# Block diagonal products as 64-wide pairs on two quarters of the array

## The chip, the cores and the metric

The kernel runs on one core of one Trainium2 chip. The metric is the device time of one launch in microseconds; the medians below are over separate runs, and the profile shows one further execution.

## The reference, cut to what matters

The program is a delta-rule attention followed by two feed-forward layers. Shapes: 4 batches, 8 heads, 768 tokens, head size 48; the layers see 3072 tokens of width 384.

```
k_n = k / (norm(k) + 1e-06)
for t in range(S):                                   # S = 768
    y[:, :, t] = einsum('bhd,bhde->bhe', q[:, :, t], state)
    v_old = einsum('bhde,bhd->bhe', state, k_n[:, :, t])
    state = state + beta_t * einsum('bhd,bhe->bhde', k_n[:, :, t], v_t - v_old)
x = y as (3072, 384)
out = sum over 4 experts of p[:, e] * (relu(x @ w1[e]) @ w2[e])      # inner width 1024
gate = 1 / (1 + exp(-(out @ w_gate)));  val = out @ w_val             # inner width 1536
return (gate * val) @ w_out
```

## The kernel before, in words

The attention is done in 12 steps of 64 tokens (`NC`, `C`). Four batches give a step two tiles (`i` = 0, 1) of 128 partitions; a tile holds two batches, one in partitions 0 to 63, the other in 64 to 127, and 8 heads lie along the free axis. Keys and queries lie transposed in `KQ` (and `YQ`, `KS`): the first batch of a tile in rows 64 to 111, the second in rows 0 to 47.

For each step, tile and head the kernel forms the Gram matrix of the 64 keys with keys and queries (`g_mm`, L318). To serve both batches in one product it first copies the keys into a block diagonal tile, `bdG` (`fill_bd`, L289 and L290), whose other blocks are zero. VectorE scales and masks the results into `LP`. From there they go through DRAM to `Lpp`, where VectorE inverts the unit triangular matrices of many heads at once, row by row (`inv_ops`, the instructions on `itmp` and `Xpp`). The first four steps invert 32-wide halves only (`INV[r][1]` is true for them); the rest inverts 64-wide. The inverse comes back through DRAM into `Xbd`, again block diagonal and 128 wide (`x_in`, `put`), and for the first four steps the off-diagonal 32x32 block comes into `Ld` (`off_in`).

The chain of one step (`chain`) is: products of keys and state (`ks_task`, L499 and L500, tile `pk`), then, for the first four steps only, two half products (`half_task`, L512: part 0 with `Xbd`, part 1 with `Ld`, tile `pu`), then the product with the inverse (`tb_task`, L521, tile `pu`), the read-out (`y_task`, tiles `py` and `yt`) and the new state (`s_task`, tile `ps`). Each is done once for a tile of 8 heads; this is called a task below. `ks_task` already works with quarters: for each head one product from rows 64 to 111 into outputs 0 to 63, and one from rows 0 to 47 into outputs 64 to 127.

The layers take most of the time: products of 128x128 weights with 512 columns (L689 into `ph`, L726 into `acc`), in float32r, with each operand split into a high and a low part. The attention's own products are float32 and show up as two records each.

The order of all instructions is fixed when the program is built. A model of time (`T`, `pe_at`, `vec_at`) goes through the layers; `plan` gives each task a due time, and `slot` and `fill` emit the due tasks between two groups of the layers' products. The model counts an attention task as 1.7 us whatever it holds, so its order doesn't depend on how the task's products are written. Before the layers begin, `startup` does steps 0 and 1's Gram matrices, those of steps 2 and 3, the inverses of steps 0 and 1 and the chain of step 0, with products on zeros (`warm`, L884) between. Every engine runs its own instructions in order. SP and GpSimd issue the DMAs.

Of the kernel before, what the change touches and what calls it, by code (L numbers as in the profile page):

```python
# [9 lines left out]
F32 = mybir.dt.float32  # L10
# [16 lines left out]
P = 128  # L27
# [57 lines left out]
def moe_delta_kernel(  # L85
# [14 lines left out]
    nc = tc.nc  # L100
# [43 lines left out]
    KQi = [KQ[:, :, i] for i in range(2)]  # L144
    KS = ap_.tile([112, 2, H, C], F32, name="KS")
    bdG = ap_.tile([112, 2, H, P], F32, name="bdG")
    YQ = ap_.tile([P, 2, 2, H, C], F32, name="YQ")
    KI = ap_.tile([P, 2, 2, H, D], F32, name="KI")
    rhsA = ap_.tile([112, 2, H, D], F32, name="rhsA")
    rhsB = ap_.tile([P, 2, H, D], F32, name="rhsB")  # L150
    V = ap_.tile([P, 2, H, D], F32, name="V")
    R = ap_.tile([P, 2, H, D], F32, name="R")
    Y = [ap_.tile([P, 2, DM], F32, name=f"Y{n}") for n in range(2)]
    YT = ap_.tile([112, KT + 1, 2, P], F32, name="YT")
    Xbd = ap_.tile([P, 2, H, P], F32, name="Xbd")
    Ld = ap_.tile([P, 2, H, P], F32, name="Ld")
    LP = [ap_.tile([P, 2, 2, H, C], F32, name=f"LP{n}") for n in range(2)]
    Lts, Pts = [t[:, 0] for t in LP], [t[:, 1] for t in LP]
    Lpp = ap_.tile([P, HC, 3 * HC], F32, name="Lpp")
# [114 lines left out]
    ld_t, od_t, xd_t, pd_t = {}, {}, {}, {}  # L274
# [7 lines left out]
    def load_kq(c):  # L282
        (q[1] or q[0]).dma_start(out=KQ, in_=kq[c])
# [1 line left out]
    def load_ks(c):  # L285
        (q[1] or q[0]).dma_start(out=KS, in_=kq[c, :, 0])

    def fill_bd(bd, t, i, eng):
        eng(out=bd[64:112, i, :, 0:C], in_=t[i][64:112, 0])  # L289
        eng(out=bd[0:48, i, :, C:P], in_=t[i][0:48, 0])  # L290

    def load_ys(c):
        if c:
            (q[1] or q[0]).dma_start(out=YQ[64:112, 0], in_=kq[c, 64:112, 1])
            (q[1] or q[0]).dma_start(out=YQ[0:C, 1], in_=kq[c, 0:C, 1])
        kv = kt[c].rearrange("p (i h d) -> p i h d", i=2, h=H)
        (q[1] or q[0]).dma_start(out=KI[0:C, 0], in_=kv[0:C])
        (q[1] or q[0]).dma_start(out=KI[C:P, 1], in_=kv[C:P])
        pd = pd_t.pop(c).rearrange("p (i h t) -> p i h t", i=2, h=H)
        q[0].dma_start(out=YQ[0:C, 0], in_=pd[0:C])  # L300
        q[0].dma_start(out=YQ[C:P, 1], in_=pd[C:P])
# [7 lines left out]
    def bank(shape, name):  # L309
        turn[0] += 1  # L310
        p, tag = free[turn[0] % len(free)]
        return p.tile(shape, F32, tag=tag, name=name)

    def g_mm(i, hg, bd, kq_t):
        pg = bank([P, 4, 2, C], "pg")
        for j in range(4):
            h = hg * 4 + j
            nc.tensor.matmul(out=pg[:, j], lhsT=bd[0:112, i, h], rhs=kq_t[i][0:112, :, h], start=True, stop=True)  # L318
        return pg

    def g_l(pg, c, i, hg):
        hs = slice(hg * 4, hg * 4 + 4)
        vec.tensor_tensor(
            out=Lts[c % 2][:, i, hs],
            in0=pg[:, :, 0],
            in1=w_all[:, 2 * c + i, hs].unsqueeze(2).to_broadcast([P, 4, C]),
            op=ALU.mult,
        )
# [9 lines left out]
    def g_raw(pg, c, i, hg):  # L338
        hs = slice(hg * 4, hg * 4 + 4)
        nc.scalar.copy(out=LP[c % 2][:, :, i, hs].rearrange("p a h t -> p h a t"), in_=pg)  # L340
# [125 lines left out]
    def put(t, p0, c0, n, src):  # L466
        q[0].dma_start(
            out=t[p0 : p0 + n, :, :, c0 : c0 + n].rearrange("p i h t -> p (i h) t"),
            in_=src.rearrange("i h j t -> j (i h) t"),
        )  # L470

    def x_in(c):
        r, c2 = INV_OF[c]
        for bp in range(2):
            if INV[r][1]:
                for a in range(2):
                    put(Xbd, bp * C + a * HC, bp * C + a * HC, HC, xd_t[r][c2, a, :, :, bp])
            else:
                put(Xbd, bp * C, bp * C, C, xd_t[r][c2, :, :, bp])

    def off_in(c):
        r, c2 = INV_OF[c]
        if INV[r][1]:
            for bp in range(2):
                put(Ld, bp * C, bp * C + HC, HC, od_t[r][c2, :, :, bp])

    def scale_v(c):
        for i in range(2):
# [13 lines left out]

    def half_task(c, i, part):
        U = Y[c % 2][:, i].rearrange("p (h d) -> p h d", h=H)
        m = P - HC if part == 0 else P
        pu = bank([P, H, D], "pu")
        for h in range(H):
            if part == 0:
                lhsT, rhs = Xbd[:, i, h, 0:m], R[:, i, h]
            else:  # L510
                lhsT, rhs = Ld[:, i, h], U[:, h]
            nc.tensor.matmul(out=pu[0:m, h], lhsT=lhsT, rhs=rhs, start=True, stop=True)  # L512
        if part == 0:
            nc.scalar.copy(out=U[0:m], in_=pu[0:m])
        else:
            vec.tensor_tensor(out=R[:, i], in0=R[:, i], in1=pu, op=ALU.subtract)

    def tb_task(c, i):
        pu = bank([P, H, D], "pu")
        for h in range(H):  # L520
            nc.tensor.matmul(out=pu[:, h], lhsT=Xbd[:, i, h], rhs=R[:, i, h], start=True, stop=True)  # L521
        wv = w_all[:, 2 * c + i].unsqueeze(2).to_broadcast([P, H, D])
        vec.tensor_tensor(out=rhsA[0:C, i], in0=pu[0:C], in1=wv[0:C], op=ALU.mult)
        vec.tensor_tensor(out=rhsB[C:P, i], in0=pu[C:P], in1=wv[C:P], op=ALU.mult)
# [249 lines left out]
    def plan(t, fn, kind=""):  # L774
        todo.append((t, len(todo), kind, fn))
# [87 lines left out]
    def plan_g(c, t):  # L863
        plan(t, lambda: load_kq(c))
        for i in range(2):
            plan(t + 12, lambda i=i: fill_bd(bdG, KQi, i, nc.scalar.copy))

        def g_task(i, hg):
            pg = g_mm(i, hg, bdG, KQi)
            g_l(pg, c, i, hg)  # L870
            g_p(pg, c, i, hg)

        for n, (i, hg) in enumerate([(0, 0), (0, 1), (1, 0), (1, 1)]):
            plan(t + 14 + 2 * n, lambda i=i, hg=hg: g_task(i, hg), "pe")
        plan(t + 23, lambda: (l_out(c), l_off(c), p_out(c)))

    def startup():
# [10 lines left out]
        KQ1 = [YQ[0:112, :, i] for i in range(2)]  # L888
# [10 lines left out]
        l_init(1)  # L899
        vec.memset(zero.bitcast(F32), 0.0)  # L900
        nc.scalar.activation(out=nt_[:, 0, 0], in_=zero[:, :H].bitcast(F32), func=AF.Sqrt)
        for i in range(2):
            nc.gpsimd.memset(bdG[0:64, i], 0.0)
            vec.memset(bdG[64:112, i, :, C:P], 0.0)
        for t in (Xbd, Ld, rhsA[C:112], rhsB[0:C], KI[C:112, 0], KI[0:C, 1], Y[0][P - HC :], Y[1][P - HC :]):
            nc.gpsimd.memset(t, 0.0)
        warm(WARM)

        def norm_one(c):
            vec.tensor_tensor(out=kn[c], in0=kn[c], in1=kn[c], op=ALU.mult)  # L910
            norm_sum(kn[c], c, 1)

        pg = {}
        norm_one(0)
        fill_bd(bdG, KQi, 0, vec.tensor_copy)
        norms(0, 1)
        fill_bd(bdG, KQi, 1, nc.scalar.copy)
        for i, hg in tasks:
            pg[0, i, hg] = g_mm(i, hg, bdG, KQi)
            g_l(pg[0, i, hg], 0, i, hg)  # L920
        l_out(0)
        l_read(0)
# [1 line left out]
        KQ3 = [t[:112, : 2 * H * C].rearrange("p (a h t) -> p a h t", a=2, h=H) for t in dec_mem[2:4]]  # L924
        for i in range(2):
            sp.dma_start(out=KQ3[i], in_=kq[3, :, :, i])
        for i in range(2):
            fill_bd(Xbd, KQ1, i, nc.scalar.copy)
        for bp in range(2):
            o = bp * C  # L930
            nc.scalar.copy(out=Ld[o : o + HC, :, :, o + HC : o + C], in_=Lts[0][o : o + HC, :, :, HC:C])
        norm_one(1)
        for i, hg in tasks[:2]:
            pg[1, i, hg] = g_mm(i, hg, Xbd, KQ1)
            g_p(pg[0, i, hg], 0, i, hg)
        norms(1, 2)
        for i, hg in tasks[2:]:
            g_p(pg[0, i, hg], 0, i, hg)
            pg[1, i, hg] = g_mm(i, hg, Xbd, KQ1)
        q[0] = pool_q  # L940
        p_out(0)
        load_v(0)
        for i, hg in tasks:
            g_l(pg[1, i, hg], 1, i, hg)
            g_p(pg[1, i, hg], 1, i, hg)
        nc.gpsimd.memset(Xbd[64:112, :, :, 0:C], 0.0)
        nc.gpsimd.memset(Xbd[0:48, :, :, C:P], 0.0)
        p_out(1)
        load_ys(0)
        scale_v(0)  # L950
# [13 lines left out]

        q[0] = pool_q
        raw = [(c, i, t) for c, t in ((2, KQi), (3, KQ3)) for i in range(2)]
        for n, (c, i, t) in enumerate(raw):
            for _, j, u in raw[: 2] if n == 0 else raw[n + 1 : n + 2] if n else []:
                fill_bd(bdG, u, j, nc.scalar.copy)
            for hg in range(2):  # L970
                g_raw(g_mm(i, hg, bdG, t), c, i, hg)
            if i:
                scale_p(c)
                p_out(c)
# [49 lines left out]
    with tc.manual_schedule():  # L1024
# [11 lines left out]
        for c in range(4, NC, 2):  # L1036
            t = dec_mem[c // 2] if c < NC - 2 else dec_mem[2]
            o = 0.7 * c - 2.0
# [23 lines left out]
        for n, (kind, b, e, s0, ns) in enumerate(PHASES):  # L1062
            nf = NF1 if kind == "m1" else NF2
            part = unit_us(kind, ns) / (2 if kind == "m1" else 3)
            h = {}
# [93 lines left out]
```

## Time and profile before

| | us |
|---|---|
| median of 3 runs | 1516.54 |
| lowest and highest | 1514.53, 1518.94 |
| the profiled execution | 1512.61 |
| its span in the profile | 1510.8 |
| mean granted clock of TensorE | 0.981 |

The span runs from the first to the last instruction that the profiler saw; the rest of the execution's time lies around it. Records of TensorE overlap: a product is recorded for longer than it holds the engine, so the spacing of starts tells what one costs. A granted clock of 1.00 is TensorE's level of 2.4 GHz, 0.50 that of 1.2 GHz.

### The profile page before, as it was taken

Reading aid. Unit: us, or ns where it says so; the run is one execution under the profiler, and the core shown is the slowest. Engines: PE = TensorE matmul, PEld = TensorE weight load, DVE = VectorE, ACT = ScalarE, POOL = GpSimd, SP = SyncE. Lnnn points to the kernel's source line nnn. Section 1 sums busy time; section 2 is a strip of 40 time slices with the busy share of each in tenths; the row PEclk is TensorE's granted clock in tenths of the full one; section 3 lists DMA queues with packets and bytes.
Section 4 is the critical chain, followed back from the end, with each engine's and each line's share of the span. In section 5 each row is a group of like instructions: output and inputs, shape, how many; then the busy total and the mean of one; then the engine's idle time right before and its main releaser. Section 6 shows DMA issues by size and latency. Waiting matters only on the chain.

```text
span 1510.8 us, 23046 instructions
## 1 busy us (share of the span) xinstructions
PE 1468.1 (97%) x8801; PEld 1222.8 (81%) x8801; DVE 1066.9 (71%) x1905; ACT 574.4 (38%) x921; POOL 264.9 (18%) x293
## 2 busy tenths in 40 slices
PE   5799899999999999999999999999999999999998
PEld 5688777888888888888888888888888888888887
DVE  8877998846888766778766778757778754444553
ACT  4045444533333334333343333343433343433343
POOL 4241457530011200012110002220001210001000
PEclk8689999999999999999999999999999999999999
DMA  8586688675443675444584435495433463333221
GB/s 231 163 260 208 222 267 266 215 202 151 150 139 109 181 189 146 140 141 128 162 208 133 133 116 165 132 225 144 133 102 106 132 163 94 123 101 108 88 94 63
DMA packets 97749, 235.50 MB, mean 156 GB/s; under 512 B 23544, under 2 KB 29816, under 8 KB 95608
## 3 DMA queue, kind: packets, MB, share of 16 engines
q1 hardware_dynamic: 87352, 195.04, 43.2%
q0 software_dynamic: 10144, 38.94, 9.9%
q8 instruction: 69, 1.13, 0.3%
q14 instruction: 40, 0.33, 0.1%
q10 hardware_dynamic: 144, 0.07, 0.0%
HBM read 202.10 MB, written 27.97 MB: 152 GB/s over the span
## 4 chain that ended last, share of the span: by engine, by line
PE 86%; DVE 8%; DMA 3%; issue 2%; ACT 1%; SPq 0%; DVEq 0%; ACTq 0%
PE ph L689 43%; PE acc L726 33%; PE pu L521 3%; PE pg L318 2%; DVE Xpp L112 1%; DVE itmp L112 1%; PE pk L499 1%; PE ps L571 1%; DMA raw<-in_wp 1%; DVE ws L112 1%; DMA ls<-LP 1%; PE yt L534 1%; DVE hlo L112 1%; PE pu L512 1%; PE yt L535 1%
## 5 line engine op out<-in xcount | busy, mean ns | idle before, releaser
L689 PE MATMUL ph<-xhi,ws 128*128 128x512 f32 (+1 forms) x2064 | 635.4, 390 | 1.5 <-ACT xhi L756 0.8
L726 PE MATMUL acc<-hhi,ws 128*128 128x512 f32 (+1 forms) x1632 | 497.2, 387 | 0.0
L689 PEld LDWEIGHTS ph<-xhi,ws 128*128 128x128 f32 x2064 | 378.4, 188 | 77.2 <-ACT xhi L589 1.3
L689 PE MATMUL ph<-xlo,ws 128*128 128x512 f32 (+1 forms) x1032 | 398.2, 386 | 0.7 <-DVE xlo L112 0.7
L726 PEld LDWEIGHTS acc<-hhi,ws 128*128 128x128 f32 x1632 | 302.0, 189 | 59.3 <-ACT hhi L696 0.3
L112 DVE TENSOR_TENSOR ws<-raw,ws 128x768 fp32r<-128x768 f32 x308 | 298.3, 970 | 60.8 <-ACT ws L190 58.1
L726 PE MATMUL acc<-hlo,ws 128*128 128x512 f32 (+1 forms) x816 | 314.5, 385 | 8.3 <-DVE hlo L112 8.2
L190 ACT CAST ws<-raw 128x768 fp32r<-128x768 f32 x308 | 253.8, 830 | 83.5 <-PE acc L726 63.8
L696 ACT ACTIVATE hhi<-ph 128x512 fp32r<-128x512 f32 (+1 forms) x200 | 116.2, 581 | 418.6 <-PE ph L689 410.9
L689 PEld LDWEIGHTS ph<-xlo,ws 128*128 128x128 f32 x1032 | 194.2, 188 | 41.8 <-DVE xlo L112 2.6
L112 DVE SCALAR_TENSOR_TENSOR hlo<-ph,hhi 128x512 fp32r<-128x512 f32 (+1 forms) x200 | 132.6, 666 | 130.6 <-ACT hhi L696 130.5
L726 PEld LDWEIGHTS acc<-hlo,ws 128*128 128x128 f32 x816 | 154.0, 189 | 40.6 <-DVE hlo L112 10.2
L112 DVE TENSOR_TENSOR itmp<-Xpp,Lpp 128x120 f32<-128x120 f32 (+27 forms) x403 | 174.3, 445 | 9.7 <-DMA Lpp<-ls 3.8
L112 DVE TENSOR_TENSOR Xpp<-Xpp,itmp 128x120 f32<-128x120 f32 (+27 forms) x403 | 176.2, 449 | 5.1
L112 DVE TENSOR_TENSOR gv<-ph,sg 128x512 f32<-128x512 f32 x72 | 49.7, 691 | 94.7 <-PE ph L689 94.6
L705 ACT CAST hhi<-gv 128x512 fp32r<-128x512 f32 x72 | 44.6, 620 | 171.7 <-DVE gv L112 171.7
L753 POOL TENSOR_TENSOR ACC<-ACC,ctmp 128x512 f32<-128x512 f32 x36 | 50.1, 1393 | 321.1 <-DVE ctmp L112 320.5
L112 DVE TENSOR_TENSOR hlo<-gv,hhi 128x512 fp32r<-128x512 f32 x72 | 51.3, 713 | 49.4 <-ACT hhi L705 49.4
L703 ACT ACTIVATE sg<-ph 128x512 f32<-128x512 f32 x72 | 43.0, 597 | 76.7 <-PE ph L689 76.7
L373 POOL DMA_DIRECT2D ld<-LP x16 | 10.7, 670 | 333.5 <-DVE LP L112 333.5
L318 PE MATMUL pg<-KQ,bdG 112*128 112x128 f32 x320 | 45.2, 291 | 15.1 <-ACT bdG L290 10.8
L318 PEld LDWEIGHTS pg<-KQ,bdG 112*128 112x128 f32 x320 | 43.6, 205 | 20.0 <-ACT bdG L290 12.4
(163 smaller groups left out, 1104.7 us busy)
## 6 DMA issues: line engine op xcount, KB each, us to landing
raw<-in_wp SPq DMA_DIRECT2D x200, 384.0 KB, 3.1
raw<-w_d SPq DMA_DIRECT2D x108, 384.0 KB, 3.5
KQ<-in_kq SPq DMA_DIRECT2D x9, 896.0 KB, 7.9
pd<-LP POOLq DMA_DIRECT2D x12, 512.0 KB, 8.1
YQ<-pd POOLq DMA_DIRECT2D x24, 256.0 KB, 7.0
Lpp<-ld POOLq DMA_DIRECT2D x8, 768.0 KB, 13.5
pe<-p_d SPq DMA_DIRECT2D x23, 256.0 KB, 4.4
dec_a<-in_wp SPq DMA_DIRECT2D x15, 384.0 KB, 4.3
```

The costliest lines, as they stand in the source:

```text
L112: return fn(*args, **kw)
L190: nc.scalar.copy(out=w[:, 0], in_=t)
L318: nc.tensor.matmul(out=pg[:, j], lhsT=bd[0:112, i, h], rhs=kq_t[i][0:112, :, h], start=True, stop=True)
L499: nc.tensor.matmul(out=pk[0:C, h], lhsT=KS[C:112, i, h], rhs=rhsA[C:112, i, h], start=True, stop=True)
L512: nc.tensor.matmul(out=pu[0:m, h], lhsT=lhsT, rhs=rhs, start=True, stop=True)
L521: nc.tensor.matmul(out=pu[:, h], lhsT=Xbd[:, i, h], rhs=R[:, i, h], start=True, stop=True)
L689: nc.tensor.matmul(out=res[q], lhsT=lt, rhs=rt, start=(k == 0 and j == 0), stop=(k == KT - 1 and j == 2))
L696: nc.scalar.activation(out=hh, in_=res[0], func=AF.Relu)
L703: nc.scalar.activation(out=sg, in_=res[0], func=AF.Sigmoid)
L705: nc.scalar.copy(out=hh, in_=gv)
L726: nc.tensor.matmul(out=acc_t[d][:, :w], lhsT=lt, rhs=rt, start=(u == 0 and j == 0), stop=(u == nf - 1 and j == 2),)
L753: (nc.vector if e == NE - 1 else nc.gpsimd).tensor_tensor(out=a, in0=a, in1=t, op=ALU.add)
```

## The change

The tile `Xbd` becomes `XT`, 64 columns wide a head in place of 128, and `Ld` shrinks likewise: both batches' blocks lie in the same columns, one in partitions 0 to 63, the other in 64 to 127. Each product with them is done by `pair_mm` as two products of 64x64, one on the rows and outputs 0 to 63, one on 64 to 127. `half_task` now copies all 128 rows of its first half product; the last 32, which it left out before, meet zeros in `Ld`.

The Gram matrices of steps 0 to 3, which `startup` does, read the keys in place (`g_mm` with `HALF`): rows 64 to 111 into outputs 0 to 63 and rows 0 to 47 into outputs 64 to 127, with no block diagonal copy. From step 4 on they stay as they were (`g_bd`). So the fills of `bdG` and `Xbd` in `startup` go, as do the clears of `Xbd` and of the last rows of `Y`; `bdG` is cleared as a whole on GpSimd.

```diff
-    Xbd = ap_.tile([P, 2, H, P], F32, name="Xbd")
-    Ld = ap_.tile([P, 2, H, P], F32, name="Ld")
+    XT = ap_.tile([P, 2, H, C], F32, name="XT")
+    Ld = ap_.tile([P, 2, H, C], F32, name="Ld")
...
+    HALF = ((slice(0, C), slice(C, 112)), (slice(C, P), slice(0, D)))
...
+    def g_mm(i, hg, kq_t):
+        pg = bank([P, 4, 2, C], "pg")
+        for j in range(4):
+            h = hg * 4 + j
+            for to, at in HALF:
+                nc.tensor.matmul(
+                    out=pg[to, j], lhsT=kq_t[i][at, 0, h], rhs=kq_t[i][at, :, h], start=True, stop=True
+                )
+        return pg
+
+    def pair_mm(out, lhsT, rhs):
+        for o in (0, C):
+            nc.tensor.matmul(out=out[o : o + C], lhsT=lhsT[o : o + C], rhs=rhs[o : o + C], start=True, stop=True)
...
-                    put(Xbd, bp * C + a * HC, bp * C + a * HC, HC, xd_t[r][c2, a, :, :, bp])
+                    put(XT, bp * C + a * HC, a * HC, HC, xd_t[r][c2, a, :, :, bp])
             else:
-                put(Xbd, bp * C, bp * C, C, xd_t[r][c2, :, :, bp])
+                put(XT, bp * C, 0, C, xd_t[r][c2, :, :, bp])
...
             if part == 0:
-                lhsT, rhs = Xbd[:, i, h, 0:m], R[:, i, h]
+                pair_mm(pu[:, h], XT[:, i, h], R[:, i, h])
             else:
-                lhsT, rhs = Ld[:, i, h], U[:, h]
-            nc.tensor.matmul(out=pu[0:m, h], lhsT=lhsT, rhs=rhs, start=True, stop=True)
+                pair_mm(pu[:, h], Ld[:, i, h], U[:, h])
...
         for h in range(H):
-            nc.tensor.matmul(out=pu[:, h], lhsT=Xbd[:, i, h], rhs=R[:, i, h], start=True, stop=True)
+            pair_mm(pu[:, h], XT[:, i, h], R[:, i, h])
...
-        for i in range(2):
-            nc.gpsimd.memset(bdG[0:64, i], 0.0)
-            vec.memset(bdG[64:112, i, :, C:P], 0.0)
-        for t in (Xbd, Ld, rhsA[C:112], rhsB[0:C], KI[C:112, 0], KI[0:C, 1], Y[0][P - HC :], Y[1][P - HC :]):
+        for t in (XT, Ld, bdG, rhsA[C:112], rhsB[0:C], KI[C:112, 0], KI[0:C, 1]):
             nc.gpsimd.memset(t, 0.0)
...
         norm_one(0)
-        fill_bd(bdG, KQi, 0, vec.tensor_copy)
         norms(0, 1)
-        fill_bd(bdG, KQi, 1, nc.scalar.copy)
         for i, hg in tasks:
-            pg[0, i, hg] = g_mm(i, hg, bdG, KQi)
+            pg[0, i, hg] = g_mm(i, hg, KQi)
             g_l(pg[0, i, hg], 0, i, hg)
...
-        for i in range(2):
-            fill_bd(Xbd, KQ1, i, nc.scalar.copy)
...
-        nc.gpsimd.memset(Xbd[64:112, :, :, 0:C], 0.0)
-        nc.gpsimd.memset(Xbd[0:48, :, :, C:P], 0.0)
...
-        for n, (c, i, t) in enumerate(raw):
-            for _, j, u in raw[: 2] if n == 0 else raw[n + 1 : n + 2] if n else []:
-                fill_bd(bdG, u, j, nc.scalar.copy)
+        for c, i, t in raw:
             for hg in range(2):
-                g_raw(g_mm(i, hg, bdG, t), c, i, hg)
+                g_raw(g_mm(i, hg, t), c, i, hg)
```

VectorE's instructions at the program's begin, both kernels against each other (`L112` is the line of a helper through which all of VectorE's instructions go; `kn` holds the keys whose norms are summed into `w_all`):

```order
 L112 MEMSET pre_lo 128x512
-L112 MEMSET bdG 48x8x64 x2
 L112 TENSOR_TENSOR kn<-kn 128x768
 L112 TENSOR_REDUCE w_all<-kn 128x16
-L112 COPY bdG<-KQ 48x8x64 x2
 L112 TENSOR_TENSOR norm_tmp<-norm_tmp 128x16
```

Two clears and two copies are gone from in front of the norms; nothing else on VectorE changes its place.

TensorE's instructions from the begin to the first product with `Ld`, before:

```order
L884 MATMUL acc_129<-pre_lo 128x512 x11
L318 MATMUL pg<-KQ,bdG 128x128 x16
L318 MATMUL pg<-YQ,Xbd 128x128 x16
L318 MATMUL pg<-KQ,bdG 128x128 x16
L318 MATMUL pg<-dec_a,bdG 128x128 x8
L318 MATMUL pg<-dec_b,bdG 128x128 x8
L979 MATMUL acc_129<-Xpp 128x512 x4
L884 MATMUL acc_129<-pre_lo 128x512 x14
L512 MATMUL pu<-R,Xbd 96x48 x16
L512 MATMUL pu<-Y_112,Ld 128x48 x8
```

and of the change (the lines are those of the changed kernel):

```order
L899 MATMUL acc_129<-pre_lo 128x512 x11
L329 MATMUL pg<-KQ 64x128 x32
L329 MATMUL pg<-YQ 64x128 x32
L329 MATMUL pg<-KQ 64x128 x32
L329 MATMUL pg<-dec_a 64x128 x16
L329 MATMUL pg<-dec_b 64x128 x16
L983 MATMUL acc_129<-Xpp 128x512 x4
L899 MATMUL acc_129<-pre_lo 128x512 x14
L336 MATMUL pu<-R,XT 64x48 x32
L336 MATMUL pu<-Y_112,Ld 64x48 x16
```

Each group keeps its place and has twice as many products, half as wide; all later tasks with `Xbd` or `Ld` are replaced in the same way, and the products of the layers between them are untouched.

## Rows read from the trace of the kernel before

**Rows 1.** The page: busy time by engine, and the granted clock in 40 slices.
```profile
PE 1468.1 (97%) x8801; PEld 1222.8 (81%) x8801; DVE 1066.9 (71%) x1905; ACT 574.4 (38%) x921; POOL 264.9 (18%) x293
...
PEclk8689999999999999999999999999999999999999
```

**Rows 2.** The page: the chain that ended last, shares of the span by engine.
```profile
PE 86%; DVE 8%; DMA 3%; issue 2%; ACT 1%; SPq 0%; DVEq 0%; ACTq 0%
```

**Rows 3.** Stages: length, busy us of PE, PEld, DVE, ACT, POOL; granted clock, DMA share, GB/s.
```profile
66.90:74.90 8.00, 7.93 (x34) 7.44 (x34) 4.84 (x18) 0.00 (x0) 0.14 (x1) 0.50 0.60 167
107.70:118.00 10.30, 10.30 (x66) 10.08 (x66) 5.56 (x11) 2.11 (x4) 2.35 (x3) 0.50 0.90 304
131.00:220.00 89.00, 81.63 (x444) 69.89 (x443) 82.38 (x167) 45.42 (x81) 38.06 (x38) 0.98 0.73 228
220.00:1510.00 1290.00, 1283.22 (x7510) 1060.05 (x7508) 883.73 (x1379) 482.15 (x757) 176.99 (x195) 1.00 0.50 145
```

**Rows 4.** Waits of TensorE from 220 us on, the longest: total us, times, longest.
```profile
PE acc L726 <- DVE hlo L112: 2.2, 1, 2.2
```

**Rows 5.** Timeline of TensorE, a task with the inverse: start, length, instruction, count.
```profile
1255.88 0.39 PE L689 MATMUL ph<-xlo,ws 128*128 128x512 f32 x1
1256.11 1.88 PE L521 MATMUL pu<-R,Xbd 128*128 128x48 f32 x16
1257.81 0.71 PE L689 MATMUL ph<-xhi,ws 128*128 128x512 f32 x2
1258.36 0.40 PE L689 MATMUL ph<-xlo,ws 128*128 128x512 f32 x1
```

**Rows 6.** Timeline of TensorE, begin and end of a task of keys and state.
```profile
1252.55 0.39 PE L726 MATMUL acc<-hlo,ws 128*128 128x512 f32 x1
1252.87 0.25 PE L499 MATMUL pk<-rhsA,KS 48*64 48x48 f32 x1
1252.87 0.25 PE L500 MATMUL pk<-rhsB,KS 48*64 48x48 f32 x1
...
1253.93 0.73 PE L689 MATMUL ph<-xhi,ws 128*128 128x512 f32 x2
1254.50 0.40 PE L689 MATMUL ph<-xlo,ws 128*128 128x512 f32 x1
```

**Rows 7.** Timeline of TensorE, a first half product and what follows.
```profile
329.94 1.48 PE L512 MATMUL pu<-R,Xbd 128*96 128x48 f32 x16
331.24 0.70 PE L726 MATMUL acc<-hhi,ws 128*128 128x512 f32 x2
```

**Rows 8.** Chain of waits, step 0's end: start, length, what.
```profile
66.37 0.56 DVE R L112
66.97 3.65 PE pu L521 x16
...
71.18 3.28 PE pu L521 x16
...
75.02 1.88 PE py L546 x32
```

**Rows 9.** Chain of waits, the opening.
```profile
7.18 0.72 DVE bdG L112
7.94 0.94 DVE bdG L112
8.92 5.39 PE pg L318 x32
...
24.44 13.73 DMA ls<-LP
```

**Rows 10.** Chain of waits, step 1.
```profile
106.22 0.47 DVE R L112
106.73 2.75 PE pu L521 x16
...
111.54 3.28 PE pu L521 x16
```

More of the change, by code (lines that the diff above doesn't have):

```diff
@@ L286, in load_ks @@
         (q[1] or q[0]).dma_start(out=KS, in_=kq[c, :, 0])
-    def fill_bd(bd, t, i, eng):
-        eng(out=bd[64:112, i, :, 0:C], in_=t[i][64:112, 0])
-        eng(out=bd[0:48, i, :, C:P], in_=t[i][0:48, 0])
     def load_ys(c):
@@ L312, in bank, with fill_bd, g_bd @@
         return p.tile(shape, F32, tag=tag, name=name)
-    def g_mm(i, hg, bd, kq_t):
+    HALF = ((slice(0, C), slice(C, 112)), (slice(C, P), slice(0, D)))
+    def fill_bd(t, i):
+        nc.scalar.copy(out=bdG[64:112, i, :, 0:C], in_=t[i][64:112, 0])
+        nc.scalar.copy(out=bdG[0:48, i, :, C:P], in_=t[i][0:48, 0])
+    def g_bd(i, hg, kq_t):
         pg = bank([P, 4, 2, C], "pg")
@@ L317, in g_mm @@
             h = hg * 4 + j
-            nc.tensor.matmul(out=pg[:, j], lhsT=bd[0:112, i, h], rhs=kq_t[i][0:112, :, h], start=True, stop=True)
+            nc.tensor.matmul(out=pg[:, j], lhsT=bdG[:, i, h], rhs=kq_t[i][0:112, :, h], start=True, stop=True)
         return pg
+    def g_mm(i, hg, kq_t):
[10 more added lines that the diff above has]
+            nc.tensor.matmul(out=out[o : o + C], lhsT=lhsT[o : o + C], rhs=rhs[o : o + C], start=True, stop=True)
     def g_l(pg, c, i, hg):
@@ L484, in off_in @@
             for bp in range(2):
-                put(Ld, bp * C, bp * C + HC, HC, od_t[r][c2, :, :, bp])
+                put(Ld, bp * C, HC, HC, od_t[r][c2, :, :, bp])
     def scale_v(c):
@@ L504, in half_task @@
         U = Y[c % 2][:, i].rearrange("p (h d) -> p h d", h=H)
-        m = P - HC if part == 0 else P
         pu = bank([P, H, D], "pu")
@@ L508, in half_task @@
             if part == 0:
-                lhsT, rhs = Xbd[:, i, h, 0:m], R[:, i, h]
+                pair_mm(pu[:, h], XT[:, i, h], R[:, i, h])
             else:
-                lhsT, rhs = Ld[:, i, h], U[:, h]
-            nc.tensor.matmul(out=pu[0:m, h], lhsT=lhsT, rhs=rhs, start=True, stop=True)
+                pair_mm(pu[:, h], Ld[:, i, h], U[:, h])
         if part == 0:
-            nc.scalar.copy(out=U[0:m], in_=pu[0:m])
+            nc.scalar.copy(out=U, in_=pu)
         else:
@@ L865, in plan_g @@
         for i in range(2):
-            plan(t + 12, lambda i=i: fill_bd(bdG, KQi, i, nc.scalar.copy))
+            plan(t + 12, lambda i=i: fill_bd(KQi, i))
         def g_task(i, hg):
-            pg = g_mm(i, hg, bdG, KQi)
+            pg = g_bd(i, hg, KQi)
             g_l(pg, c, i, hg)
@@ L926, in startup @@
             sp.dma_start(out=KQ3[i], in_=kq[3, :, :, i])
-        for i in range(2):
-            fill_bd(Xbd, KQ1, i, nc.scalar.copy)
         for bp in range(2):
             o = bp * C
-            nc.scalar.copy(out=Ld[o : o + HC, :, :, o + HC : o + C], in_=Lts[0][o : o + HC, :, :, HC:C])
+            nc.scalar.copy(out=Ld[o : o + HC, :, :, HC:C], in_=Lts[0][o : o + HC, :, :, HC:C])
         norm_one(1)
         for i, hg in tasks[:2]:
-            pg[1, i, hg] = g_mm(i, hg, Xbd, KQ1)
+            pg[1, i, hg] = g_mm(i, hg, KQ1)
             g_p(pg[0, i, hg], 0, i, hg)
@@ L938, in startup @@
             g_p(pg[0, i, hg], 0, i, hg)
-            pg[1, i, hg] = g_mm(i, hg, Xbd, KQ1)
+            pg[1, i, hg] = g_mm(i, hg, KQ1)
         q[0] = pool_q
```

## The prediction

> **What bounds the kernel now.** I read the page first. TensorE is busy for 97% of the span and no other engine for more than 71% [rows 1]. The chain that ended last agrees: 86% of it is TensorE and 8% VectorE [rows 2]. A busy share alone is weak evidence, because products overlap, so I cut the span by stage [rows 3]. From 220 us to 1510 us TensorE is busy for 1283.22 of 1290 us at the full granted clock, VectorE for 883.73, ScalarE for 482.15. The longest wait of TensorE in that stretch is a single one of 2.2 us [rows 4]. So in this stretch every microsecond that TensorE's instruction stream gets shorter comes off the end. Before it the picture is another: from 131 to 220 us VectorE is busy for 82.38 of 89 us, and in 66.9 to 74.9 us and 107.7 to 118 us TensorE works at a granted clock of 0.50 [rows 3], which is its level of 1.2 GHz. A saving there is worth what the chain of work makes of it.
>
> The order of instructions on every engine is written out beforehand and the change leaves it as it was but for what it replaces. So I can cost each replaced group where it stands.
>
> **1. Products with the inverse, steps 2 to 11 (20 tasks of 8 heads).** A task has 8 products, 16 records in the profile (two passes of float32). In the timeline around 1256 us [rows 5] I read starts, since records overlap. The last product before the task starts 0.23 us ahead of it, which is the usual spacing; the task holds the engine from 1256.11 to 1257.81, 1.70 us; and the two products after it take 0.55 us (1257.81 to 1258.36), where twice the usual spacing is 0.46. Together 2.48 us. That is 106 ns a record, although only 48 columns are streamed: a 128-wide weight load for each sets the pace.
>
> The new form is 32 records in 16 pairs, each a 64x64 block on its own quarter. The trace of before has the same form already, in the product of keys and state [rows 6]: rows 64 to 111 into outputs 0 to 63 beside rows 0 to 47 into outputs 64 to 127, stationary 48x64, 48 columns streamed, 32 records a task. Both records of a pair start at 1252.87. The task starts 0.32 us after the product ahead of it, lasts 1.06 us to 1253.93, and the two products behind it take 0.57 us: 1.95 us. The change's pairs have 64 rows where these have 48, and lie on the other diagonal; I take the row's value for them. Saved: 2.48 - 1.95 = 0.53 us a task, 20 x 0.53 = 10.6 us.
>
> **2. The off-diagonal block, steps 2 and 3 (4 tasks).** Same shape as above before and after: 4 x 0.53 = 2.1 us.
>
> **3. The first half products, steps 2 and 3 (4 tasks).** These load only 96 columns. They hold the engine from 329.94 to 331.24, 1.30 us [rows 7], with the edges of rows 5 (0.23 and 0.55): 2.08 us. Saved 0.13 each, 0.5 us.
>
> Items 1 to 3 lie where TensorE has no slack: **13.2 us**.
>
> At the edges row and rule have to be weighed. The pairs start late by 0.32 - 0.23 = 0.09 us and the first products behind them lose another 0.57 - 0.55 = 0.02 us [rows 5, 6]; this is inside the 1.95 us. The Trainium skill, "TensorEngine Tiling (Array Packing)", section Key Properties, says that changing the tiling mode drains TensorE. That rule speaks against this change, which adds such switches; what it would make of the sum is the fourth rival below. The trace agrees that a switch costs something, about 0.11 us a task.
>
> **4. Opening, before the inverse of step 0.** VectorE copies two blocks for the first Gram matrix, 7.18 to 8.88 us, and TensorE starts on it at 8.92 [rows 9]. Both copies go, and the first half of the keys has landed by 7.18, so the first Gram products start up to 1.74 us sooner. The Gram products as such I cost at nothing: 64 records of quarters with 128 columns streamed against 32 whole ones; a whole one takes 5.39/32 = 168 ns there [rows 9], part of it at the lower clock, and a pair that costs no more than a whole one leaves the time as it is. If pairs cost double, 5.4 us more work would stand against it, and nothing would be gained here. What the start is worth depends on the transfers: the chain shows a 13.73 us transfer of the next blocks, 24.44 to 38.17 us [rows 9]. I take **1.7 us**; ends: 0 (the transfers stay where they are) and 3.4 (the norms, queued on VectorE behind the copies, give as much again). The other fills on ScalarE, the two clears on GpSimd and the two clears of Y lie beside these transfers, and I cost their going at nothing. GpSimd's clear of the block diagonal tile moves behind those of XT and Ld; it is needed first for step 4, far behind.
>
> **5. Step 0's products with the inverse.** After VectorE's last subtraction (66.37) come two tasks at the lower clock, 3.65 and 3.28 us, and then the first read-out at 75.02 [rows 8]. That read-out has 64-wide pairs at the same clock: 32 records in 1.88 us. With 1.88 for each task, 1.77 + 1.40 = **3.2 us** are saved; ends: 0 (the read-out then waits for VectorE's scaling) and 4.8 (1.06 each, as in rows 6 at the higher clock). The tasks of half products before it wait on no path: VectorE works through the inverse of step 1 until 66.37.
>
> **6. Step 1.** Its half products run before VectorE is done with the norms; its next subtraction starts at 106.22 [rows 10]. I cost them at nothing; what covers them is that VectorE work, and without it they would give some 2 us more. The two tasks behind it take 2.75 and 3.28 us [rows 10]; with 1.88 each: 0.87 + 1.40 = **2.3 us**; ends 0 and 3.9 (1.06 each again).
>
> Where these stalls go: VectorE's norms at 102 to 106 us and the transfers ahead of them are late next, and they move with the start.
>
> **Sum.** 13.2 + 1.7 + 3.2 + 2.3 = 20.4 us. The profiled execution took 1512.61 us (span 1510.8), so it would take 1492.2; the median shown, 1516.54, stands 3.9 us above it, so 1496.1, say **1496 us**. Its own range: 13.2 + 0 gives 1503.3, 13.2 + 3.4 + 4.8 + 3.9 = 25.3 gives 1491.2. The runs shown spread by 2 us to each side, so 1489 to 1505.5.
>
> **Rivals.**
> - *The start gives nothing* (0.17). VectorE is busy for 93% of 131 to 220 us [rows 3]; if its work or the transfers are not freed sooner, items 4 to 6 are waited away there. Against it: VectorE has 5.56 of 10.3 us in 107.7 to 118, so it waits for TensorE just there. Left: 13.2 us, 1503.
> - *The pairs don't run side by side* (0.04), the case on the other side. Place: every changed task. Then a task lasts 2 x 1.06 = 2.12 us, with its edges 3.01 against 2.48 and 2.08: 24 x 0.53 + 4 x 0.93 = 16.4 us more, steps 0 and 1 at 3.76 a task 2.1 us more, and nothing at the opening: 18.5 us slower, 1535. It decides from a pair spacing of (2.48 - 0.32 - 0.57)/16 = 99 ns on; rows 6 have 66. Against it: those pairs do start together, and the read-out, with all rows in use and only the columns halved, runs in pairs too [rows 8].
> - *The clock* (0.06). With shorter work in the start, the level of 2.4 GHz may come back later. One stretch like 107.7 to 118 us costs about half its 10.3 us [rows 3]; two more of them leave 10.1 us of gain, 1506. Against it: TensorE worked at 1.2 GHz through most of the start anyway.
> - *Full drains at the edges* (0.06). By that mechanism a task would start only when the product ahead had ended, 0.39 us after its start [rows 6], 0.07 later than the pairs of rows 6 do, and the next product only after the last pair's 0.25 us, at most 0.18 more than a pair's spacing of 0.07: up to 0.25 us more a task, 28 x 0.25 = 7 us, 1503. This is the rule of the page named above, taken at its fullest; the pairs of rows 6 have both edges in them and pay 0.11, so I give it little.
> - *More than that* (0.05): the start gives its upper ends, with the 2 us of the covered half tasks: 27.3 us, 1489.
>
> The forecast itself gets 0.62. The range that holds 8 in 10 takes in the start that gives nothing, the clock and the full drains: 1488 to 1508. A change of 0.3%, about 4.5 us, is what a measurement of this kernel can tell from none. Faster by more: 0.91, from all cases but the serial pairs, less a rest for a rival that comes together with another; same 0.04; slower 0.05.
>
> **What will show it.** Right: between 260 and 1265 us each task of the inverse lasts 1.06 us, with 32 records in pairs that start together, and the stretch from 220 us on is 13 us shorter. Item 4 is right if the first Gram product starts near 7.2 us, item 5 if the first read-out follows VectorE's subtraction by about 5.5 us in place of 8.65, item 6 if the two tasks of step 1 take under 2 us each. Wrong: pairs that start one after the other, a start that ends no sooner, or new stretches of 0.50 in the granted clock.

## The result, and the profile after

The changed kernel takes 1497.3 us in the median of 4 runs (1497.07 to 1498.53); the kernel before took 1515.53 in 4 runs beside them (1514.44 to 1518.94). The ratio is 0.9886, with a 95% interval of 0.9869 to 0.9902: some 18 us less. The profiled execution took 1497.07 us with a span of 1495.3, against 1512.61 and 1510.8 before. So the two traces stand 15.5 us apart and the medians 18.2: the profiled execution of before was a quick one, 2.9 us under its median. What is worked out below from the two traces adds up to 15.5.

The page of the kernel after: busy time by engine, the granted clock in 40 slices, and the shares of the chain that ended last.

```profile
PE 1440.4 (96%) x9569; PEld 1183.7 (79%) x9569; DVE 1063.0 (71%) x1901; ACT 566.4 (38%) x907; POOL 259.3 (17%) x288
...
PEclk8789999999999999999999999999999999999999
...
PE 85%; DVE 8%; DMA 3%; issue 2%; ACT 1%; SPq 0%; DVEq 0%; ACTq 0%
```

Beside [rows 1, 2]: TensorE has 768 records more and is busy for 27.7 us less. It is still the bound, and the other engines did not move much. The granted clock fell below full in the same slices as before.

The stages of the kernel after. The first and the last two windows answer to [rows 3]; the second is the stretch at the lower clock in step 1. Columns as in [rows 3].

```profile
66.90:74.90 8.00, 8.00 (x102) 6.20 (x100) 7.45 (x21) 0.48 (x1) 1.08 (x2) 0.50 0.69 160
104.20:111.00 6.80, 3.78 (x41) 3.69 (x41) 6.17 (x14) 2.84 (x5) 0.56 (x1) 0.50 1.03 349
131.00:220.00 89.00, 81.81 (x429) 69.27 (x429) 82.78 (x163) 43.59 (x78) 39.88 (x42) 0.98 0.74 236
220.00:1495.00 1275.00, 1266.07 (x7941) 1035.11 (x7939) 878.61 (x1373) 481.60 (x756) 174.10 (x192) 1.00 0.51 146
```

From 220 us to the end TensorE is busy for 1266.07 of 1275 us; before, it was 1283.22 of 1290. Its work shrank by 17.2 us and the stretch by 15: idle time grew from 6.8 to 8.9 us. (The window begins in work that lies up to 3.8 us apart in the two kernels, so for the sum a better mark is taken below, the first half product of step 2.) The stretch at 0.50 in step 1 lasts 6.8 us, from 104.2 to 111.0, in place of 10.3 [rows 3].

Timeline of TensorE in the kernel after, a task with the inverse in step 10, the counterpart of [rows 5]: start, length, instruction, count.

```profile
1244.77 0.39 PE L704 MATMUL ph<-xlo,ws 128*128 128x512 f32 x1
1245.08 1.14 PE L336 MATMUL pu<-R,XT 64*64 64x48 f32 x32
1246.15 0.73 PE L741 MATMUL acc<-hhi,ws 128*128 128x512 f32 x2
1246.72 0.40 PE L741 MATMUL acc<-hlo,ws 128*128 128x512 f32 x1
```

The task has 32 records and holds the engine from 1245.08 to 1246.15, 1.07 us in place of 1.70. It starts 0.31 us after the product ahead, and the next two take 0.57 us. Together 1.95 us: to the hundredth what [rows 6] gave for pairs with 48 rows on the other diagonal. Neither the 64 rows nor the diagonal made a difference. Taken record by record, the two of a pair start 7 ns apart, and the next pair starts 58 ns behind: the sign that the prediction named.

The same view in step 2, where the tasks stand early (the bracket is the idle time ahead, and what ended it):

```profile
283.42 1.13 PE L336 MATMUL pu<-R,XT 64*64 64x48 f32 x32 [0.23 <-DVE R L112]
...
286.75 1.14 PE L336 MATMUL pu<-R,XT 64*64 64x48 f32 x32
...
289.77 0.40 PE L704 MATMUL ph<-xlo,ws 128*128 128x512 f32 x1
291.59 0.33 PE L549 MATMUL yt<-YQ,rhsA 112*64 112x64 f32 x4 [1.42 <-issue]
```

Here the tasks are as short, but TensorE waits 0.23 us for VectorE ahead of the first and 1.42 us ahead of the read-out of the first (`yt`), which reads what VectorE makes of that task (`rhsA` and `rhsB`, written up to 291.49 us; the read-out starts at 291.59, so this wait too is VectorE's, though the view names no releaser). VectorE in this place, first of the kernel after:

```profile
282.81 0.55 DVE L112 TENSOR_TENSOR R<-R,pu 128x384 f32<-128x384 f32 x1
...
290.37 0.54 DVE L112 TENSOR_TENSOR rhsA<-pu,w_all 64x384 f32<-64x384 f32 x1
290.93 0.56 DVE L112 TENSOR_TENSOR rhsB<-pu,w_all 64x384 f32<-64x384 f32 x1
```

and of the kernel before:

```profile
286.60 0.55 DVE L112 TENSOR_TENSOR R<-R,pu 128x384 f32<-128x384 f32 x1
...
294.17 0.54 DVE L112 TENSOR_TENSOR rhsA<-pu,w_all 64x384 f32<-64x384 f32 x1
294.73 0.56 DVE L112 TENSOR_TENSOR rhsB<-pu,w_all 64x384 f32<-64x384 f32 x1
```

All three stand 3.79 to 3.80 us sooner than before. The start had given just that by then (the first half product of step 2 begins at 269.72 us in place of 273.51). So between 270 and 292 us VectorE's queue sets the pace, and what TensorE saved there became waiting.

The start, in the chain of waits of the kernel after; its counterparts are [rows 8] to [rows 10].

```profile
7.14 1.96 PE pg L329 x32
9.13 1.99 PE pg L329 x32
...
13.05 4.57 DMA ls<-LP
...
17.77 6.47 DMA Lpp<-ls
24.26 13.46 DMA ls<-LP
...
65.97 0.56 DVE R L112
...
66.57 1.95 PE pu L336 x32
...
69.24 1.88 PE pu L336 x32
...
71.84 1.88 PE py L561 x32
...
90.17 10.41 DMA raw<-in_wp
...
106.62 0.56 DVE R L112
...
107.22 1.95 PE pu L336 x32
...
111.28 1.06 PE pu L336 x32
```

The reader sees a gain that comes and goes. The first Gram products start 1.8 us sooner and end after 4 us, and their first blocks are written at 11.58 us in place of 14.75. Of these 3.2 us only 1.8 are the copies; the rest is mostly the clock, which stood at 0.50 from 8.8 to 12.2 us in the trace of before (the first 32 records took 5.39 us, the next 32 at 1.00 took 4.08) and at 1.00 in this one. But the second transfer of blocks on the chain lands at 24.26 + 13.46 = 37.72 us, where it landed at 38.17 before [rows 9]: 3.2 us became 0.45. VectorE's subtraction for step 0 starts 0.40 us sooner [rows 8]. The two tasks behind it last 1.95 and 1.88 us, and the first read-out follows the subtraction by 5.87 us in place of 8.65: 2.8 us won. Then a load of weights, issued at 90.17, lands at 100.58 us, where before one issued at 92.32 landed at 100.09 (92.32 + 7.77). The product of step 1 therefore starts at 107.22, half a microsecond later than before [rows 10]. The load was issued 2.2 us sooner but was 10.41 us on its way in place of 7.77; why it took longer, no run shows. All that the start had won is gone by then.

### The profile page after: what moved, and what is told of

The parts are those of the page before. It is cut to its first block, busy times and chain, and to the rows that moved or that the text cites. A ratio compares the mean times of both kernels' runs of the same rounds, so it can differ in the third digit from the quotient of the medians.

```text
span 1495.3 us, 24548 instructions
## 1 busy us (share of the span) xinstructions
PE 1440.4 (96%) x9569; PEld 1183.7 (79%) x9569; DVE 1063.0 (71%) x1901; ACT 566.4 (38%) x907; POOL 259.3 (17%) x288
## 4 chain that ended last, share of the span: by engine, by line
PE 85%; DVE 8%; DMA 3%; issue 2%; ACT 1%; SPq 0%; DVEq 0%; ACTq 0%
PE ph L704 43%; PE acc L741 34%; PE pu L336 2%; DVE Xpp L112 2%; PE pg L321 1%; DVE itmp L112 1%; DMA ls<-LP 1%; PE pk L516 1%; DMA raw<-in_wp 1%; DVE ws L112 1%; PE ps L586 1%; PE yt L549 1%; DVE hlo L112 1%; DMA Lpp<-ls 1%; DVE dec_b L112 1%
## 5 line engine op out<-in xcount | busy, mean ns | idle before, releaser
L112 DVE TENSOR_TENSOR ws<-raw,ws 128x768 fp32r<-128x768 f32 x308 | 298.9, 972 | 58.0 <-ACT ws L190 55.2
L112 DVE SCALAR_TENSOR_TENSOR hlo<-ph,hhi 128x512 fp32r<-128x512 f32 (+1 forms) x200 | 132.5, 666 | 130.4 <-ACT hhi L711 130.1
L112 DVE TENSOR_TENSOR itmp<-Xpp,Lpp 128x120 f32<-128x120 f32 (+27 forms) x403 | 174.1, 444 | 13.5 <-DMA Lpp<-ls 7.6
L112 DVE TENSOR_TENSOR Xpp<-Xpp,itmp 128x120 f32<-128x120 f32 (+27 forms) x403 | 175.7, 448 | 5.1
L112 DVE TENSOR_TENSOR gv<-ph,sg 128x512 f32<-128x512 f32 x72 | 49.7, 690 | 89.0 <-PE ph L704 88.9
L112 DVE TENSOR_TENSOR hlo<-gv,hhi 128x512 fp32r<-128x512 f32 x72 | 51.4, 714 | 49.4 <-ACT hhi L720 49.4
L336 PEld LDWEIGHTS pu<-R,XT 64*64 64x64 f32 x1024 | 35.0, 143 | 28.4 <-DVE R L112 18.2
L112 DVE TENSOR_TENSOR ctmp<-acc,pe 128x512 f32<-128x512 f32 x54 | 37.1, 687 | 27.5 <-PE acc L741 27.5
## 6 DMA issues: line engine op xcount, KB each, us to landing
Lpp<-ld POOLq DMA_DIRECT2D x8, 768.0 KB, 13.2
```

The costliest lines, as they stand in the source:

```text
L112: return fn(*args, **kw)
L336: nc.tensor.matmul(out=out[o : o + C], lhsT=lhsT[o : o + C], rhs=rhs[o : o + C], start=True, stop=True)
```

## The experiments

In each group the runs of the kernel before stood beside the experiments on the same chip: a median of 1516.19 us for four of them (the Gram matrices alone, the pairs alone, the column halves, the late Gram matrices), 1514.59 for the other four.

**Which half of the change gives the time.** First the Gram matrices alone: the kernel before, with the Gram products of steps 0 to 3 on quarters of the keys in place, and the products with the inverse left 128 wide.

```diff
-            pg[0, i, hg] = g_mm(i, hg, bdG, KQi)
+            pg[0, i, hg] = g_mm(i, hg, KQi)
```

> The kernel before with only the opening's change: Gram matrices of steps 0 to 3 read the keys in place, without block diagonal copies; the products with the inverse stay 128 wide. Theory (the gain of the change lies in the products with the inverse; the opening's is waited away, because the transfer of step 1's blocks lands at 37.7 us after the change where it landed at 38.2 before): within 2 us of the kernel before, 1513 to 1517 us, and the first subtraction of step 0's chain behind the inverse still at 65.5 to 66.5 us. Rival (the opening carries a share of its own): 1508 to 1512 us.

Measured: 1516.22 us (12 runs), ratio 0.9999 (0.9989 to 1.0009). The opening alone is worth nothing, to a thousandth. The time came as expected; the subtraction did not, it starts at 68.53 us in this trace (the last section comes back to this).

Then the counterpart: the kernel after, with block diagonal copies for the Gram matrices of steps 0 to 3, as before.

```diff
-            pg[0, i, hg] = g_mm(i, hg, KQi)
+            pg[0, i, hg] = g_bd(i, hg, KQi)
...
-            pg[1, i, hg] = g_mm(i, hg, KQ1)
+            pg[1, i, hg] = g_bd(i, hg, KQ1, bd1)
```

> The changed kernel with the opening put back: block diagonal copies for the Gram matrices of steps 0 to 3, while the products with the inverse and its off-diagonal block run as pairs. Theory (all of the gain is the pairs): 1497 to 1499 us, each task with the inverse 1.06 us behind 260 us. Rival (the opening carries a share): 1501 to 1505 us.

Measured: 1499.8 us (5 runs), ratio 0.9883 (0.9867 to 0.99), that is, the whole gain of the change within the interval. The median lies 0.8 us above the range of the theory and 1.2 below that of the rival, so by itself this run leaves room for a small share of the opening; the first run, whose interval is 1.5 us to each side, leaves none that can be measured. Together: the time comes from the 64-wide pairs.

**What makes a pair run side by side.** In the first of two kernels each product with the inverse keeps the block diagonal tile and all 128 rows, and only its columns are cut in two. (It has the opening of the first experiment, and its first half products write all 128 outputs.)

```diff
+    def col_mm(out, lhsT, rhs):
+        for o in (0, C):
+            nc.tensor.matmul(out=out[o : o + C], lhsT=lhsT[:, o : o + C], rhs=rhs, start=True, stop=True)
```

> As the run with only the opening changed, but each product with the 128-wide inverse or off-diagonal block is cut in two by columns alone: all 128 rows into outputs 0 to 63, then all 128 rows into outputs 64 to 127. Theory (a task is paced by the weight loads, and halves of the columns load side by side): the task lasts 1.06 us as with quarters, 1496 to 1500 us. Rival (records run side by side only if their rows differ too): pairs one after the other, 1.7 us a task or more and the edges on top, 1515 us or more.

Measured: 1498.63 us (4 runs), ratio 0.9882 (0.9863 to 0.99), in the range of the theory. The timeline of TensorE of this kernel, one task:

```profile
1249.56 1.14 PE L335 MATMUL pu<-R,Xbd 128*64 128x48 f32 x32
1250.63 0.72 PE L744 MATMUL acc<-hhi,ws 128*128 128x512 f32 x2
```

The task holds the engine for 1.07 us, as the quarters do, and its records start in the same rhythm, 7 ns within a pair and 58 ns from pair to pair. So it isn't the smaller array quarter that counts: two column halves suffice, though both use every row. The Trainium skill, "TensorE: Matmul & The Clock Gate", section Part 3: Packing small matmuls (The mechanism), says that a weight load overlaps with products in flight only when their row groups differ. This trace doesn't bear that out: the row groups here are the same, and the pair still takes 67 ns (1.07 / 16), against the 106 ns of one 128-wide record [rows 5] and the 112 ns of two on the same quarter (next run).

In the second kernel everything is as after, but the order: the 8 heads of a task first all on the lower quarter, then all on the upper.

```diff
+    def halves_mm(pu, lhsT, rhs):
+        for o in (0, C):
+            for h in range(H):
+                nc.tensor.matmul(
+                    out=pu[o : o + C, h], lhsT=lhsT[o : o + C, h], rhs=rhs[o : o + C, h], start=True, stop=True
+                )
```

> The changed kernel with the products of a task in another order: all 8 heads on the quarter of rows 0 to 63 first, then all 8 on the quarter of rows 64 to 127, so that neighbours use the same quarter. Theory (the gain comes from two neighbours loading weights side by side): neighbours on one quarter go one after the other, 32 records at 58 to 66 ns, 1.86 to 2.1 us a task in place of 1.06, 28 tasks on the busy stretch: 22 to 29 us slower than the changed kernel, 1519 to 1526 us. Rival (half as many columns make the loads short enough by themselves): 1.06 us a task and 1497 to 1499 us.

Measured: 1522.38 us (4 runs), ratio 1.0045 (1.0027 to 1.0063). Its timeline, one task:

```profile
292.47 1.87 PE L523 MATMUL pu<-R,XT 64*64 64x48 f32 x32
294.27 0.72 PE L743 MATMUL acc<-hhi,ws 128*128 128x512 f32 x2
```

The same 32 records now take 1.80 us, 56 ns each, one after the other. A 64-wide record alone is thus quicker than a 128-wide one (106 ns), but two in a row are not (112): narrower loads by themselves give nothing. The time is above the kernel before's, and 25 us behind the kernel after. The products are the same, so the gain lies in what stands next to each: neighbours on the same quarter run one after the other, neighbours on different columns side by side (in the run ahead of this one with all rows shared). The expectation on the time held, and the task came out a little shorter than its lower end. This is the rival with serial pairs, made real: it does end on the other side. The forecast for that rival was 1535, because it doubled the 1.06 us of a task to 2.12, where 1.80 came.

A kernel with the rows halved and all 128 columns kept, two products added into the same outputs, wasn't tried, so nothing is shown on neighbours that differ in their rows alone.

**Why the later Gram matrices stay block diagonal.** The kernel after, with quarters for the Gram matrices of steps 4 to 11 too, and without the copies for them.

```diff
-        for i in range(2):
-            plan(t + 12, lambda i=i: fill_bd(KQi, i))
...
-            pg = g_bd(i, hg, KQi)
+            pg = g_mm(i, hg, KQi)
```

> The changed kernel with the Gram matrices of steps 4 to 11 in quarters too, and without their block diagonal copies on ScalarE. Theory (with 128 columns streamed a pair takes about 0.12 us, as in the opening of the changed kernel, where a whole block diagonal record takes 0.10 to 0.11): 8 pairs of a task of 4 heads last 0.95 to 0.98 us in place of 0.81, the edges add 0.1, 32 tasks: 6 to 9 us slower than the changed kernel, 1503 to 1507 us. Rival (paced by the weight loads like the products with the inverse): 0.53 us a task, 32 x 0.17 = 5 us faster, 1491 to 1493 us.

Measured: 1504.8 us (5 runs), ratio 0.9924 (0.9909 to 0.9938): 7.5 us slower than the kernel after, as the theory said. TensorE in one Gram task of this kernel:

```profile
421.65 0.39 PE L704 MATMUL ph<-xlo,ws 128*128 128x512 f32 x1
421.97 1.09 PE L329 MATMUL pg<-KQ 48*64 48x128 f32 x16
422.99 0.74 PE L741 MATMUL acc<-hhi,ws 128*128 128x512 f32 x2
```

and in the kernel after, with the block diagonal copy:

```profile
422.39 0.40 PE L741 MATMUL acc<-hlo,ws 128*128 128x512 f32 x1
422.62 1.05 PE L321 MATMUL pg<-KQ,bdG 112*128 112x128 f32 x8
423.43 0.72 PE L704 MATMUL ph<-xhi,ws 128*128 128x512 f32 x2
```

With 128 columns streamed a pair takes 1.02 / 8 = 128 ns, and a whole record 0.81 / 8 = 101 ns. There is nothing to win, and the edges come on top. A task costs some 0.3 us more (0.21 in itself, 0.09 ahead of it); over the 24 tasks behind 271 us that is 7 us. The copies on ScalarE that it saves win nothing back there. From the first half product of step 2 to the end of the span it is 1504.8 - 271.93 = 1232.9 us in place of 1225.6: 7.3 more. The two spans are 9.5 us apart; the other 2.2 us were there already at step 0's subtraction (68.19 us in place of 65.97; see the last section).

**Where the start's gain went.** Two suspects were in the trace of the kernel after: 1.8 MB of keys and queries for steps 2 and 3, queued ahead of small transfers of blocks at about 13 to 24 us; and SyncE's queue at 84 to 90 us. The first kernel moves the loads behind the stores of step 1's blocks.

```diff
-        load_kq(2)
...
-            sp.dma_start(out=KQ3[i], in_=kq[3, :, :, i])
...
         l_off(1)
+        load_kq(2)
...
+            sp.dma_start(out=KQ3[i], in_=kq[3, :, :, i])
         l_read(1)
```

> The changed kernel with three loads moved in SP's queue: the keys and queries of steps 2 and 3 (1.8 MB) are issued behind the stores of step 1's blocks, not ahead of them. Theory (the opening's gain was lost because those stores, issued from 21 us on, stood behind the loads and landed at 37.7 us): the stores land before 32 us, the inverse of step 1 starts 3 to 4 us sooner, and the first subtraction behind it comes at 62 to 63.5 us in place of 66.0; of that 2 to 4 us reach the end, 1493 to 1496 us. Rival (the weight loads at 90 to 106 us set the pace of the start again, whatever comes before): the subtraction comes sooner, the time stays at 1496.5 to 1499 us.

Measured: 1495.41 us (4 runs), ratio 0.9869 (0.9852 to 0.9885), not to be told from the kernel after. Its chain (of an execution of 1500.49 us, the longest of the four):

```profile
31.95 9.60 DMA Lpp<-ls
...
65.11 0.56 DVE R L112
...
89.28 11.12 DMA raw<-in_wp
```

The blocks had landed by 31.1 us in place of 37.7, but the next transfer on the chain then took 9.60 us in place of 4.15. It landed at 41.55 us, where it had landed at 42.48, and so the subtraction came at 65.11 us in place of 65.97, and not at 62 to 63.5. The median lies in the range of the theory, but its mechanism fell in part: the next transfer took over the wait (that it competes with the moved loads is likely, but no run shows it). And the weight load again ended what was left: the product of step 1 starts at 107.04 us.

The second suspect. SyncE's queue in the kernel after:

```profile
84.01 0.39 SPq L182 DMA_DIRECT2D raw<-in_wp  x1
89.09 0.38 SPq L632 DMA_DIRECT2D dec_a<-in_kt  x1
89.52 0.60 SPq L683 DMA_DIRECT2D pe<-p_d  x1
90.17 0.42 SPq L182 DMA_DIRECT2D raw<-in_wp  x1
```

The queue stands from 84.4 to 89.1 us at a load of norm keys, which waits until its tile has been used for the keys loaded before; the weight loads wait behind it. This kernel gives that load a tile of its own.

```diff
+    kn_last = ap_.tile([P, 4 * DM], F32, name="kn_last")
...
-            t = dec_mem[c // 2] if c < NC - 2 else dec_mem[2]
+            t = dec_mem[c // 2] if c < NC - 2 else kn_last
...
-                back["dec"].append((o + 0.6, "", lambda t=t: norm_load(t, NC - 2)))
+                back["dec"].append((o + 0.6, "", lambda: norm_load(kn_last, NC - 2)))
```

> The changed kernel with a tile of its own for the keys of steps 10 and 11 that are read for the norms (in the room that the narrower tiles left), so that SP's queue doesn't stand until 89 us for VectorE and ScalarE to be done with the tile that they shared. Theory (that wait delays the weight load that ends at 100.6 us and through it the products of step 1): the weight load is issued 2 to 5 us sooner and step 1's product with the inverse starts at 103 to 105.5 us in place of 107.2; 1493.5 to 1496 us. Rival (the DMA engines are full from 90 to 110 us, so an earlier issue lands no sooner): 1497 to 1499 us.

Measured: 1493.64 us (4 runs), ratio 0.9853 (0.9831 to 0.9875). The same queue:

```profile
82.87 0.42 SPq L633 DMA_DIRECT2D kn_last<-in_kt  x1
...
84.76 0.55 SPq L183 DMA_DIRECT2D raw<-in_wp  x1
```

and TensorE at the tasks of step 1:

```profile
102.07 1.13 PE L337 MATMUL pu<-R,XT 64*64 64x48 f32 x32 [1.96 <-DVE R L112]
...
104.40 1.14 PE L337 MATMUL pu<-R,XT 64*64 64x48 f32 x32
```

The weight load is issued at 84.76 us and not at 90.17, and lands at 95.4 us and not at 100.6. The product of step 1 starts at 102.07 and not at 107.22, and both tasks last 1.07 us, since the granted clock is 1.00 from 100 to 120 us. By step 2 some of this is waited away: its first half product starts at 267.34 us, 2.4 sooner than after. The theory held: the time lies in its range, and issue and product came even sooner than it said. The interval of the time overlaps the kernel after's, so it is the trace that decides. The held load matters twice, though: its own keys also come late, and VectorE's reduction of them waited 3.57 us in the kernel after and 0.37 here. The run doesn't tell the two apart.

Both edits above at once:

> Both of the edits of the last two runs in one kernel. Theory (two waits in a row on one chain, so the gains add): 1490 to 1494 us. Rival (one takes what the other gives): no better than the better of the two, 1493.5 to 1497 us.

Measured: 1491.25 us (4 runs), ratio 0.9842 (0.9826 to 0.9859), which lies clear below the kernel after's interval. The first half product of step 2 starts at 264.93 us, 4.8 sooner than after. From there to the end of the span it is 1490.9 - 264.9 = 1226.0 us here and 1225.6 in the kernel after, so what is won ahead of step 2 comes off the end. The expectation held. This version beats both kernels.

## Why the prediction was right, and where it was not

The median forecast was 1496 and came out at 1497.3. The sum was 20.4 us against the profiled execution and the two traces stand 15.5 us apart; the medians, 18.2. Taken step by step:

- **Items 1 to 3, 13.2 us.** The mark is the first half product of step 2. From there to the end of the span it was 1510.8 - 273.5 = 1237.3 us and is 1495.3 - 269.7 = 1225.6: **11.7 us**. The price of a task was right to the hundredth (1.95 us with its edges). What failed is the sentence that from 220 us on TensorE has no slack. It holds from about 292 us: from the read-out at 291.59 (296.09 before) to the end the change gives 11.0 us, where the items forecast 10.9 for steps 3 to 11. The tasks of step 2 lie between 270 and 292, beside VectorE's queue, and their saving became waits of 0.23 and 1.42 us. The stage was cut at a round number and judged by its average; the timeline of VectorE around these very tasks would have shown it.
- **The edges.** The rows were weighed right against full drains: 0.11 us a task stood in the rows and came, and the full drains did not.
- **Item 4, the opening, 1.7 us: 0.4 in the trace, and nothing measurable.** The sign of it, the first Gram product near 7.2 us, was seen (7.14), and the first blocks were even written 3.2 us sooner, in part by the clock. The step that failed is that the transfers would move along. They were named as what the start's worth depends on; the lower end, 0, was the right value. The experiment with the opening alone shows it.
- **Item 5, 3.2 us: 2.8 at its place** (5.87 us from subtraction to read-out, where 5.5 was the sign), right in mechanism and nearly in price; the products on zeros behind each task took 0.72 us in place of 0.56. But it didn't last: the weight load took it all by 107 us. Behind step 0 the prediction named VectorE's norms and the transfers ahead of them as late next, and supposed that they move with the start. They moved by half a microsecond the other way.
- **Item 6, 2.3 us: 4.3.** From 0.5 us behind where the first task starts to 3.8 ahead where the second read-out ends (117.01 us, 120.79 before). The two tasks themselves won 3.0 us (1.95 and 1.06 in place of 2.75 and 3.28 [rows 10]); the prediction had taken the lower clock for both, and the second already ran at the higher. The other 1.3 came up to the end of the first read-out, since the stretch at 0.50 ended at 111.0 us and not at 118.0: that read-out took 1.07 us, where it had taken 1.59.

In the two traces the start gave 0.4 + 2.8 - 3.7 + 4.3 = 3.8 us, where 7.2 was forecast, and the long part 11.7, where it was 13.2: 4.9 us less together. The median still came out right to 1.3 us, and that is luck: a second error stands against the first. The prediction added 3.9 us from the profiled execution to the median, as before; the profiled execution of after lies 0.2 us below its median. Where such differences arise, the traces show in part. The run with the loads moved has the longest of its four executions in its trace: its first half product of step 2 starts at 272.83 us, and the rest takes as long as in the kernel after (1225.9 and 1225.6 us). With the Gram matrices alone the span is 5.5 us longer than that of before, the first half product of step 2 starts 5.2 us later (278.66), and the rest takes the same (1237.6 and 1237.3 us). Here the difference lies ahead of step 2. It doesn't always: with the pairs alone and with the column halves the rest takes 1229.4 and 1229.8 us. In step 3 of these two traces TensorE waits 2.0 and 2.7 us for VectorE, behind a load of weights that took 14.5 and 15.5 us, and the granted clock is at 0.50 for a short stretch near 333 us. So an execution of before that happens to be quick makes the change look smaller in the traces than it is in the medians.

Of the rivals, the one in which the start gives nothing (1503) was half true; clock and drains did not come in this kernel; serial pairs were shown to need another order of the products.

## What to carry to other kernels

Where a task is a row of small float32 products with few columns streamed, cut the stationary side into column halves and let neighbours in the stream use different ones: 8 products of 128 x 48 went from 1.70 to 1.07 us, while the same quarters in the other order took 1.80. Don't do it where many columns are streamed: at 128 of them the pair costs more than the whole. And before a saving at the start of a kernel is counted, follow the chain to the next load, and look at what its queue is standing at: here one shared tile held the weight loads for 4.7 us.

## What the runs showed that was not expected

- Column halves that share all rows run side by side as well as diagonal quarters do (1.07 us a task), and neighbours on the same quarter don't at all (56 ns each).
- In step 0 the clock's return to 2.4 GHz did not come sooner for less work: the stretch at 0.50 ended at 80.3 us in the kernel after and at 80.4 before, though the tasks in it were halved (with the column halves, at 76.9). In step 1 it began 3.5 us sooner after the change and ended 7 us sooner, and with the shared tile gone there was none. What decides it is not shown.
- The first 64 Gram records lasted 3.96 us in the kernel after and 7.09 in two of the experiments (the Gram matrices alone, and the late Gram matrices), with the same products. The opening of the kernel after, and of the Gram matrices alone:

```profile
1.47 4.51 PE L899 MATMUL acc<-pre_lo 128*128 128x512 f32 x11 [1.47 <-DVE pre_lo L112]
7.14 3.96 PE L329 MATMUL pg<-KQ 48*64 48x128 f32 x64 [1.16 <-DMA KQ<-in_kq]
```

```profile
1.47 5.06 PE L900 MATMUL acc<-pre_lo 128*128 128x512 f32 x11 [1.47 <-DVE pre_lo L112]
7.51 7.09 PE L328 MATMUL pg<-KQ 48*64 48x128 f32 x64 [0.98 <-DMA KQ<-in_kq]
```

The views give a granted clock of 1.00 in both places, but in those two traces the readings of the clock begin only at about 14.4 us (at 5.2 us in the kernel after), and a stretch without a reading counts as 1.00. The spacing of starts speaks for the lower level: from the second on the products on zeros start 427 ns apart to the last one, where in the kernel after the last two follow at 302 and 230 ns; and a Gram pair takes 222 ns, against 118 in the same trace behind 14.4 us. So it is the clock, as far as the spacing tells; why it rose 9 us later is open. The kernel with the late Gram matrices has the same opening as the kernel after, and its subtraction of step 0 came at 68.19 us in place of 65.97: an execution can lose 2.2 us there. This is a part of the spread between executions.
